# Splitting the first gather of an expert layer: table rows early, token numbers and gathers later

## The chip, the cores and the metric

The kernel runs on 1 core of one Trainium2 chip. The metric is device microseconds (us) of one execution. The core has five engines with an instruction list each: TensorE (PE in the profile; its weight loads are PEld), VectorE (DVE), ScalarE (ACT), GpSimd (POOL) and SyncE (SP, whose queue of transfers is SPq). An engine works through its own list in order and waits on semaphores for the others. A transfer that a later instruction on the same list needs is therefore also a wait for everything behind that instruction.

## The reference

Three layers are computed, all in float32, on 1536 tokens of 512 numbers.

```
x = attention(q, k, v)            # a band of 32 keys, and 24 block sums, per head
x = leaky(x @ w_in) @ w_out       # "first MoE": 512 -> 2048 -> 512, leaky(h) = max(0.01 h, h)
noisy = x @ w_gate + log1p(exp(x @ w_noise)) * noise
top2 = the two largest of the 8 experts for each token, weights = softmax of the two
out[token] += weight * (relu(x[token] @ w1[e]) @ w2[e])     # "second MoE", for both experts
```

The second MoE needs x gathered by expert: which tokens an expert has is known only once the routing of these tokens is done.

## The kernel before, in words

**First MoE.** The 1536 tokens are six groups of 256 (g = 0 to 5) and the 2048 hidden columns are 16 blocks of 128 (f). One pair (g, f) is a step; there are 96, and the last group, g = 5, is steps 80 to 95. Of one step, `l1` (L412) does 12 matmuls into a PSUM bank H0 or H1 (by the parity of f) and the leaky maximum (L424 on ACT, L426 on DVE); `l1b` (L429) cuts the result in two parts, `gh` by ACT (L433) and the rest `gl = t - gh` (L434) by GpSimd or VectorE; `l2` (L437) adds it into the accumulators `acc` with six matmuls, two with gh and one with gl for each half of the tokens. On TensorE the six of step s come after the twelve of step s+2. Which engine makes gl is a table entry: `e_gl<step>=1` is GpSimd from SBUF, 0 is VectorE, in place in the PSUM bank (L425, L434), which is then free for step s+2 only once gl is made.

**Routing.** When a group is through, `x2_out` writes its rows to DRAM (`x2d`, L454), `route_a` transposes them, `route_b` computes the two top experts, and `route_c` (L519) computes a place for each token and scatters (token number, weight) into a table in DRAM, `tabd`, with four indirect transfers that GpSimd issues (L545). The table was filled with a large number before.

**Second MoE.** Work comes in units of 210 or 420 table rows. The first, unit 0, is 210 rows of expert 0, and it takes tokens of groups 0 to 4 only: an offset (`route_off`, L553) keeps the last group's tokens out of its rows. `gather` (L781) loads a unit's rows of the table with a transfer on SP (L785, tile `tbs`), makes valid token numbers `gi` of them on GpSimd (L787), and gathers the tokens' rows with indirect transfers that GpSimd issues (L794, tile `xg`). `xg_t` (L806) transposes them, and `m1` (L817) is the first matmul of the expert. Its weights come by `load_piece` (L161): a 512 KB load on SP into one of three buffers (L171, L173), then a split into two parts, the high one by ACT (L156), the low one by VectorE (L157). The eight pieces of expert 0 are called e01 (first matrix) and e02 (second).

**What sets the order.** Before the last part, each piece of work is put at a step number, a float, by `at_step` (L579); the numbers are the table `PL` (L44). Work is issued in the order of these numbers, and a scheduler places it from there on each engine's list. `xo`, `ra`, `rb`, `rc` are the steps of `x2_out` and the three routing parts of a group, counted from the group's end; `lp` those of the weight pieces. So what an engine does next is fixed when the program is built, and a late semaphore holds everything behind it.

In the rows below, tiles have no numbers; in the lists of instructions `gl_7`, `gh_10`, `lt_9`, `h_11` are those of column block 7, 10, 9, 11 of group 5, that is of steps 87, 90, 89 and 91.

Of the kernel before, what the change touches and what calls it, by code (L numbers as in the profile page):

```python
# [31 lines left out]
NG = N // G  # L32
NT = N // P
NF = FF // P
# [34 lines left out]
          e_gl49=1, e_gl5=1, e_gl50=1, e_gl51=0, e_gl52=0, e_gl53=1, e_gl54=1, e_gl55=1, e_gl56=0, e_gl57=1, e_gl58=1,  # L69
          e_gl59=0, e_gl6=1, e_gl60=0, e_gl61=1, e_gl62=0, e_gl63=0, e_gl64=1, e_gl65=0, e_gl66=1, e_gl67=1, e_gl68=1,  # L70
          e_gl69=0, e_gl7=1, e_gl70=1, e_gl71=0, e_gl72=1, e_gl73=0, e_gl74=1, e_gl75=1, e_gl76=0, e_gl77=0, e_gl78=1,
          e_gl79=0, e_gl8=1, e_gl80=1, e_gl81=0, e_gl82=1, e_gl83=1, e_gl84=0, e_gl85=1, e_gl86=0, e_gl87=1, e_gl88=1,
          e_gl89=1, e_gl9=1, e_gl90=1, e_gl91=1, e_gl92=1, e_gl93=0, e_gl94=1, e_gl95=0, e_kr0=1, e_kr1=1, e_kr2=1,
          e_kr3=1, e_lo0=0, e_lo1=0, e_lo10=1, e_lo11=0, e_lo12=0, e_lo13=0, e_lo14=0, e_lo15=0, e_lo16=1, e_lo17=0,
          e_lo18=0, e_lo19=1, e_lo2=1, e_lo20=0, e_lo21=1, e_lo22=1, e_lo23=1, e_lo24=1, e_lo25=1, e_lo26=1, e_lo27=1,
          e_lo28=1, e_lo29=0, e_lo3=1, e_lo30=1, e_lo31=1, e_lo4=1, e_lo5=1, e_lo6=0, e_lo7=1, e_lo8=1, e_lo9=1,
# [8 lines left out]
          go50=-6.482, go51=-1.899, go52=7.046, go53=-0.034, kt00=1, kt01=0, kt10=1, kt100=1, kt101=1, kt11=1,  # L85
          kt110=0, kt111=0, kt120=0, kt121=0, kt130=1, kt131=0, kt20=1, kt21=0, kt30=1, kt31=0, l1b=2.039, l2=2.48,
          lp0=79.959, lp1=91.15, lp2=94.615, lp3=98.503, lp4=86.197, lp5=99.558, lp6=93.633, lp7=104.712, lw=-6.736,
          lws=0.593, lx=6.628, lxs=0.591, ra0=3.084, ra1=4.274, ra2=4.727, ra3=3.079, ra4=3.418, rb0=8.597, rb1=6.781,
          rb2=9.519, rb3=4.048, rb4=4.635, rc0=15.468, rc1=11.776, rc2=13.732, rc3=6.323, rc4=6.881, tg10a=2, tg10b=2,
          tg10c=3, tg10d=1, tg10e=3, tg11a=1, tg11b=2, tg11c=0, tg11d=3, tg11e=3, tg12a=1, tg12b=2, tg12c=0, tg12d=2,  # L90
          tg12e=2, tg13a=0, tg13b=2, tg13c=3, tg13d=2, tg13e=1, tg20a=1, tg20b=1, tg20c=1, tg20d=1, tg20e=0, tg21a=0,
          tg21b=0, tg21c=1, tg21d=0, tg21e=1, tg22a=0, tg22b=0, tg22c=1, tg22d=1, tg22e=0, tg23a=1, tg23b=1, tg23c=0,
# [4 lines left out]
          tgW16=0, tgW17=1, tgW18=0, tgW19=1, tgW2=0, tgW20=1, tgW21=8, tgW22=8, tgW23=8, tgW24=1, tgW25=0, tgW26=0,  # L97
          tgW27=8, tgW28=8, tgW29=8, tgW3=8, tgW30=8, tgW31=8, tgW4=8, tgW5=8, tgW6=8, tgW7=0, tgW8=8, tgW9=8, vl=0,
          w0=12, wk0=1, wk1=2, wk2=1, wk3=10, x0=-49.567, xo0=1.881, xo1=-22.198, xo2=3.458, xo3=-4.929, xo4=-10.997,
          xo5=5.591)  # L100


C_ID, C_MASK, C_IOTA, C_THR = 0, 128, 128 + 3 * NK, 136 + 3 * NK
# [24 lines left out]
def attention_moe_kernel(ctx: ExitStack, tc: tile.TileContext, q, k, v, w_in, w_out, w_gate, w_noise, noise, w1, w2,  # L128
# [390 lines left out]
    def route_c(g):  # L519

        written.add(("r", g))
        xi, oh, sel, pl, gate, sl = rt.pop(g)
        ps = bank("R", f"pos{g}")
        nc.tensor.matmul(ps[:, :E], tri, sel[:, 0, :], start=True, stop=False)
        nc.tensor.matmul(ps[:, :E], ones, selp, start=False, stop=True)
        nc.tensor.matmul(ps[:, E:2 * E], tri, sel[:, 1, :], start=True, stop=False)
        nc.tensor.matmul(ps[:, E:2 * E], ones, sel[:, 0, :], start=False, stop=False)
        nc.tensor.matmul(ps[:, E:2 * E], ones, selp, start=False, stop=True)
        nc.vector.tensor_scalar(sl[:, 1, :], sl[:, 0, :], 1.0, 1e-9, op0=ALU.add, op1=ALU.add)
        nc.vector.reciprocal(gate[:, :, 0], sl[:, 1, :])  # L530
        nc.vector.tensor_mul(gate[:, :, 1], gate[:, :, 0], sl[:, 0, :])
        nc.gpsimd.tensor_copy(pl[:, :, :, 0], tid[:, 2 * g:2 * g + 2, None].to_broadcast([P, 2, 2]))
        pos = ps[:, :2 * E].rearrange("p (t e) -> p t e", t=2)
        if g == NG - 1:
            pf = rp.tile([P, 2, E], F32, tag="pf", name="pf")
            nc.vector.tensor_add(pf, pos, off[:, None, :].to_broadcast([P, 2, E]))
            pos = pf
        nc.vector.tensor_mul(oh, oh, pos[:, :, None, :].to_broadcast([P, 2, 2, E]))
        nc.vector.tensor_reduce(sl[:, 2:4, :].rearrange("p a b -> p (a b)").rearrange("p (t k) -> p t k", t=2), oh, axis=AX.X, op=ALU.add)
        si = rp.tile([P, 2, 2], I32, tag="si", name=f"si{g}")  # L540
        nc.vector.scalar_tensor_tensor(si, xi, float(TS), sl[:, 2:4, :], op0=ALU.mult, op1=ALU.add)
        done = []
        for t in range(2):
            for j in range(2):
                i = nc.gpsimd.indirect_dma_start(out=tabd, out_offset=IOA(ap=si[:, t, j:j + 1], axis=0), in_=pl[:, t, j, :],  # L545
                                                 in_offset=None)
                for d in done:
                    tc.declare_no_dep(i.ins, d.ins, reason="every token and expert has a table row of its own")
                done.append(i)
        for t in range(2):  # L550
            nc.vector.tensor_add(selp, selp, sel[:, t, :])
# [27 lines left out]
    def at_step(s, fn, *args):  # L579
        events.setdefault(s, []).append((fn, args))  # L580
# [189 lines left out]
        at_step(PL[f"lp{i}"], load_piece, 0, i)  # L770
    at_step(20, routing_consts)
    at_step(48, zero_out)
    at_step(NG * NF - 9, route_off)

# [1 line left out]
    ex = {}  # L778
    mp = None

    def gather(u):  # L781
        e, r0, nj = units[u]
        assert all(("r", g) in written for g in range(NG - 1 + (u > 0)))
        tb = tbs[:, u, :nj, :]
        nc.sync.dma_start(tb, tabd[e * TS + r0:e * TS + r0 + nj * SLOTS, :].rearrange("(p j) c -> p j c", j=nj))  # L785
        gi = rp.tile([SLOTS, nj], I32, tag="gi", bufs=3, name=f"gi{u}")
        nc.gpsimd.tensor_scalar(gi, tb[:, :, 0], (N if u else N - G) - 1, None, op0=ALU.min)  # L787
        if u:
            x = mp.tile([SLOTS, nj, DM], F32, tag="xg", name=f"xg{u}")
        else:  # L790
            x = pa.tile([SLOTS, nj, DM], F32, tag="qn", bufs=1, name=f"xg{u}")
        xg = [x[:, j, :] for j in range(nj)]
        for j in range(nj):
            nc.gpsimd.indirect_dma_start(out=xg[j], out_offset=None, in_=x2d if u else x2d[:N - G, :], in_offset=IOA(ap=gi[:, j:j + 1], axis=0))  # L794
        ex[u] = dict(tb=tb, gi=gi, xg=xg, e=e, nj=nj, n=nj * SLOTS)
# [92 lines left out]
            tc.declare_no_dep(i.ins, o.ins, reason="an expert has each token once")  # L888
        d["out"].append(i)

    at_step(NG * NF - 7, gather, 0)
    for c in range(KD):
        at_step(NG * NF - 4 + c, xg_t, 0, c)

    pool_free = False
    for s in sorted(events):
# [30 lines left out]
    m1(0, 2)  # L927
    second(0, 1)
    route_c(last)
    gather(1)  # L930
    m1(0, 3)
    second(0, 2)
# [12 lines left out]
    for u in range(1, nu):  # L945
        end = u == nu - 1
        for f in range(NFE):
            m1(u, f)
            if f == 0 and not end:
                gather(u + 1)  # L950
            if units[u][0] + 1 < E and f < 7:
                load_piece(units[u][0] + 1, f)
            if f == 1 and u > 1:
                second(u - 1, NFE - 1)
                if not rows[u - 1]:
                    out_sb(u - 1)
# [97 lines left out]
```

## Time and profile before

| | |
|---|---|
| time, median of 3 runs | 745.65 us (741.72 to 747.62) |
| time of the profiled execution | 744.94 us |
| span of that execution, first to last instruction | 743.2 us |
| PE busy | 717.1 us, 96% of the span |
| DVE busy | 391.0 us, 53% |
| ACT busy | 302.3 us, 41% |
| POOL busy | 212.7 us, 29% |
| granted TensorE clock, mean | 0.994 of full speed |
| chain of work that ended last, by engine | PE 82%, DMA 5%, DVE 4%, POOL 3% |

Busy shares are means over the whole span. The profiled execution is one; its time has the 1.74 us around its span in it. PE is busy nearly all the time and carries 82% of the chain that ends last, so what can be won without taking matmuls away is where PE stands still, or runs at a lower granted clock.

### The profile page before, as it was taken

What the parts mean: (1) busy time and instruction counts of PE and PEld (TensorE: products, weight loads), DVE (VectorE), ACT (ScalarE), POOL (GpSimd) and SP (SyncE); (2) the same over time, 40 slices, a digit from 0 to 9 for tenths busy, and PEclk for the clock granted to TensorE, in tenths of its full rate; (3) what the DMA queues carried; (4) which work ended last, traced back from release to release, by engine and by line L of the source; (5) the groups of instructions that cost most, each with busy time, mean ns of one, the idle gap of its engine ahead of it and who ended that gap; (6) DMA issues with size and microseconds to landing.
All of it is one profiled execution on the core that took longest, in us unless ns stands there. A gap on an engine that the chain in (4) does not pass through costs nothing.

```text
span 743.2 us, 13515 instructions
## 1 busy us (share of the span) xinstructions
PE 717.1 (96%) x5240; PEld 633.0 (85%) x5240; DVE 391.0 (53%) x967; ACT 302.3 (41%) x727; POOL 212.7 (29%) x237
## 2 busy tenths in 40 slices
PE   7999999999999999999979999999999999999996
PEld 4577888777888888889869879999999999999984
DVE  3989979855533553332434455455454645454311
ACT  2568656644424544333344145332423333343210
POOL 0212722621143113131240242333324232233132
PEclk9999999999999999999989999999999999999999
DMA  9986454472630120100241257655555546563021
GB/s 249 250 237 179 85 155 163 122 161 50 199 54 30 30 54 2 58 1 1 86 138 56 88 178 233 191 140 161 171 171 163 184 143 182 168 180 124 12 79 48
DMA packets 78993, 92.41 MB, mean 124 GB/s; under 512 B 45254, under 2 KB 54982, under 8 KB 78920
## 3 DMA queue, kind: packets, MB, share of 16 engines
q1 hardware_dynamic: 70728, 72.13, 34.8%
q0 software_dynamic: 8192, 19.33, 8.7%
q8 instruction: 43, 0.70, 0.4%
q14 instruction: 30, 0.25, 0.1%
HBM read 78.62 MB, written 13.40 MB: 124 GB/s over the span
## 4 chain that ended last, share of the span: by engine, by line
PE 82%; DMA 5%; DVE 4%; POOL 3%; ACT 2%; issue 2%; SPq 2%; POOLq 0%; DVEq 0%; ACTq 0%
PE eh L827 19%; PE h L421 16%; PE acc L446 15%; PE eacc L846 15%; PE eacc L866 5%; PE sps L335 2%; DMA early<-in_moe_w_in_dram 2%; PE xgps L813 2%; PE yps L878 1%; PE vps L371 1%; PE aps L356 1%; DMA vn<-in_v_dram 1%; PE vsps L273 1%; PE lg L479 1%; POOL tabd L545 1%
## 5 line engine op out<-in xcount | busy, mean ns | idle before, releaser
L830 ACT ACTIVATE egh<-eh 128x420 fp32r<-128x420 f32 (+1 forms) x72 | 34.7, 482 | 187.6 <-PE eh L827 181.5
L831 DVE SCALAR_TENSOR_TENSOR egl<-eh,egh 128x420 fp32r<-128x420 f32 (+1 forms) x72 | 39.3, 546 | 126.9 <-ACT egh L830 120.9
L434 POOL TENSOR_TENSOR gl<-lt,gh 128x256 fp32r<-128x256 f32 x63 | 47.8, 763 | 167.1 <-ACT gh L433 139.4
L424 ACT ACTIVATE lt<-h 128x256 f32<-128x256 f32 x96 | 36.4, 381 | 68.8 <-PE h L421 59.6
L885 POOL DMA_INDIRECT out_dram<-ag,tbs x32 | 31.9, 996 | 112.5 <-DVE ag L884 100.7
L421 PE MATMUL h<-xh,w0h 128*128 128x256 f32 x192 | 56.2, 293 | 0.5 <-ACT w0h L156 0.4
L421 PE MATMUL h<-xh,w16h 128*128 128x256 f32 x192 | 55.8, 291 | 0.7 <-DVE lt L426 0.4
L421 PE MATMUL h<-xl,w0h 128*128 128x256 f32 x192 | 55.0, 287 | 0.0
L421 PE MATMUL h<-xl,w16h 128*128 128x256 f32 x192 | 54.9, 287 | 0.0
L421 PE MATMUL h<-xh,w16l 128*128 128x256 f32 x192 | 54.7, 285 | 0.0
L421 PE MATMUL h<-xh,w0l 128*128 128x256 f32 x192 | 54.2, 283 | 0.5 <-POOL w0l L157 0.5
L794 POOL DMA_INDIRECT xg<-x2d,gi x32 | 35.8, 1118 | 50.4 <-PE xgps L813 41.9
L426 DVE TENSOR_TENSOR lt<-h,lt 128x256 f32<-128x256 f32 x63 | 26.5, 420 | 40.0 <-ACT lt L424 37.3
L446 PE MATMUL acc<-w17h,gl 128*128 128x512 f32 x96 | 39.2, 408 | 6.1 <-POOL gl L434 5.3
L342 ACT ACTIVATE sm<-sm,st 128x120 f32<-128x120 f32 x96 | 36.8, 385 | 16.8 <-DVE st L340 16.7
L433 ACT ACTIVATE gh<-lt 128x256 fp32r<-128x256 f32 x63 | 26.1, 415 | 37.0 <-PE acc L446 29.2
L802 POOL DMA_INDIRECT ag<-out_dram,gi x28 | 31.8, 1134 | 32.8 <-DMA out_dram<-ag,tbs 19.4
L446 PE MATMUL acc<-w1h,gh 128*128 128x512 f32 x96 | 39.6, 414 | 0.0
L421 PEld LDWEIGHTS h<-xh,w16h 128*128 128x128 f32 x192 | 36.7, 191 | 3.4 <-DVE lt L426 0.9
L446 PE MATMUL acc<-w17h,gh 128*128 128x512 f32 x96 | 39.4, 410 | 0.0
L421 PEld LDWEIGHTS h<-xh,w0h 128*128 128x128 f32 x192 | 36.2, 188 | 3.7 <-DVE lt L426 0.6
L446 PE MATMUL acc<-w17l,gh 128*128 128x512 f32 x96 | 38.8, 404 | 0.0
(304 smaller groups left out, 2092.9 us busy)
## 6 DMA issues: line engine op xcount, KB each, us to landing
e<-in_moe_w_dram SPq DMA_DIRECT2D x64, 512.0 KB
early<-in_moe_w_in_dram SPq DMA_DIRECT2D x8, 512.0 KB
early<-in_moe_w_out_dram SPq DMA_DIRECT2D x8, 512.0 KB
raw<-in_moe_w_in_dram SPq DMA_DIRECT2D x8, 512.0 KB
raw<-in_moe_w_out_dram SPq DMA_DIRECT2D x8, 512.0 KB
vw<-in_v_dram SPq DMA_DIRECT2D x20, 192.0 KB
vn<-in_v_dram SPq DMA_DIRECT2D x8, 384.0 KB
qn<-in_q_dram SPq DMA_DIRECT2D x12, 256.0 KB
```

The costliest lines, as they stand in the source:

```text
L342: nc.scalar.activation(sm[:, i, :], sm[:, i, :], AF.Exp, bias=st[:, i:i + 1], scale=-1.0, accum_out=st[:, 4 + i:5 + i])
L421: nc.tensor.matmul(ps[:, :G], a[:, c, c0:c0 + P], x[:, c, :], start=n == 0, stop=n == 3 * KD - 1)
L424: nc.scalar.activation(t, ps[:, :G], AF.Copy, scale=0.01)
L434: (nc.gpsimd if PL[f"e_gl{g * NF + f}"] else nc.vector).tensor_sub(gl, t, gh.bitcast(F32))
L446: nc.tensor.matmul(accs[g, t], a[:, t * P:(t + 1) * P], w[:, f % 8, :], start=f == 0 and n == 0, stop=f == NF - 1 and n == 2)
L794: nc.gpsimd.indirect_dma_start(out=xg[j], out_offset=None, in_=x2d if u else x2d[:N - G, :], in_offset=IOA(ap=gi[:, j:j + 1], axis=0))
L827: nc.tensor.matmul(ps[:, :w], a[:, c, f * P:(f + 1) * P], x[:, c, :], start=n == 0, stop=n == 3 * KD - 1)
L830: nc.scalar.activation(gh, ps[:, :w], AF.Relu)
L831: nc.vector.scalar_tensor_tensor(gl, ps[:, :w], 0.0, gh.bitcast(F32), op0=ALU.max, op1=ALU.subtract)
L846: nc.tensor.matmul(ps, a[:, f, c * P:(c + 1) * P], x, start=f == 0 and n == 0, stop=f == NFE - 1 and n == 2)
L866: nc.tensor.matmul(d["acc", j][:SLOTS, :], a[:, j * SLOTS:(j + 1) * SLOTS], w[:, f, :], start=f == 0 and n == 0, stop=f == NFE - 1 and n == 2)
L885: i = nc.gpsimd.indirect_dma_start(out=out, out_offset=IOA(ap=d["tb"][:, j, 0:1], axis=0), in_=y, in_offset=None, bounds_check=N - 1, oob_ ...
```

## The change

`gather` is cut in two. The new function `table` holds the load of the table rows on SP; `gather` keeps the token numbers and the gathers on GpSimd. For the first unit, the table load is put at step 87.2 and the gather at step 90.2; both were at step 89 before. For the other units the two are called one after the other, as before. With it go changes in the table of numbers: the three routing parts of group 4 (`ra4`, `rb4`, `rc4`) are put 0.8 to 1.1 steps earlier, `route_off` at 86.6 (was 87), the four `xg_t` of the first unit at 92.6, 93.4, 94.2 and 95.0 (were 92 to 95), and the gl of steps 87, 88 and 89 is made by VectorE.

```diff
-          ... e_gl86=0, e_gl87=1, e_gl88=1,
-          e_gl89=1, ...
+          ... e_gl86=0, e_gl87=0, e_gl88=0,
+          e_gl89=0, ...
-          ... ra4=3.418, ... rb4=4.635, ... rc4=6.881, ...
+          ... ra4=2.6, ... rb4=3.7, ... rc4=5.8, ...
-          xo5=5.591)
+          xo5=5.591, ro=86.6, tb=87.2, ga=90.2, xg=92.6, xgs=.8)
...
-    at_step(NG * NF - 9, route_off)
+    at_step(PL["ro"], route_off)
...
-    def gather(u):
+    def table(u):
+
         e, r0, nj = units[u]
         assert all(("r", g) in written for g in range(NG - 1 + (u > 0)))
         tb = tbs[:, u, :nj, :]
         nc.sync.dma_start(tb, tabd[e * TS + r0:e * TS + r0 + nj * SLOTS, :].rearrange("(p j) c -> p j c", j=nj))
+
+    def gather(u):
+
+        e, r0, nj = units[u]
+        tb = tbs[:, u, :nj, :]
         gi = rp.tile([SLOTS, nj], I32, tag="gi", bufs=3, name=f"gi{u}")
         nc.gpsimd.tensor_scalar(gi, tb[:, :, 0], (N if u else N - G) - 1, None, op0=ALU.min)
...
-    at_step(NG * NF - 7, gather, 0)
+    at_step(PL["tb"], table, 0)
+    at_step(PL["ga"], gather, 0)
     for c in range(KD):
-        at_step(NG * NF - 4 + c, xg_t, 0, c)
+        at_step(PL["xg"] + PL["xgs"] * c, xg_t, 0, c)
...
     route_c(last)
+    table(1)
     gather(1)
...
+                table(u + 1)
                 gather(u + 1)
```

How this stands on the engines' lists. GpSimd, from the scatter of group 4's table rows (L545) on, before:

```order
L545 DMA tabd<-pl_4558,si_4632 13312x2 x4
L434 TENSOR_TENSOR gl_7_4719<-lt_7_4653,gh_7_4720 128x256
L434 TENSOR_TENSOR gl_8_4745<-lt_8_4684,gh_8_4746 128x256
L787 TENSOR_SCALAR gi_4714<-tbs 105x2
L794 DMA xg_4716<-x2d,gi_4714 105x512 x2
L434 TENSOR_TENSOR gl_9_4771<-lt_9_4710,gh_9_4772 128x256
L434 TENSOR_TENSOR gl_10_4808<-lt_10_4742,gh_10_4809 128x256
```

and after the change:

```order
L434 TENSOR_TENSOR gl_5_4661<-lt_5_4575,gh_5_4662 128x256
L545 DMA tabd<-pl_4532,si_4600 13312x2 x4
L793 TENSOR_SCALAR gi_4744<-tbs 105x2
L800 DMA xg_4746<-x2d,gi_4744 105x512 x2
L434 TENSOR_TENSOR gl_10_4801<-lt_10_4737,gh_10_4802 128x256
L434 TENSOR_TENSOR gl_11_4834<-lt_11_4768,gh_11_4835 128x256
```

The first gl behind the token numbers and the gathers was that of step 89; it is that of step 90 now, and between the scatter and the token numbers GpSimd has nothing else.

SP's list around the table load (4630, 4775, 4849, 4884 are pieces of expert 0's weights), the piece of the difference:

```order
-L173 DMA e_4610<-in_moe_w_dram 128x2x512
+L173 DMA e_4630<-in_moe_w_dram 128x2x512
 L171 DMA e_4775<-in_moe_w_dram 128x1024
+L786 DMA tbs<-tabd 105x4
 L173 DMA e_4849<-in_moe_w_dram 128x2x512
-L785 DMA tbs<-tabd 105x4
 L171 DMA e_4884<-in_moe_w_dram 128x1024
```

The table load, which waits for the scatter, stands ahead of weight piece 4849 now, and behind it before.

ACT's list after the change, around weight piece 4884:

```order
L433 ACTIVATE gh_9_4772<-h_9_4698 128x256
L156 ACTIVATE e02h<-e_4849 128x1024
L424 ACTIVATE lt_10_4737<-h_10_4724 128x256
L156 ACTIVATE e01h<-e_4884 128x1024
L433 ACTIVATE gh_10_4802<-lt_10_4737 128x256
L424 ACTIVATE lt_11_4768<-h_11_4755 128x256
```

These six stand in the order that they had before, but that a weight piece has come between lt of block 11 and its gh (the next row): the high part of piece 4884 is ahead of gh of step 90 in both. The gh of step 89 is read from PSUM now.

## Rows read from the trace of the kernel before

**Rows 1.** The longest wait of PE: line, waited for; us, times, longest.

```profile
PE acc L446 <- POOL gl L434: 5.3, 1, 5.3
```

**Rows 2.** The timeline of PE: start us, us, instruction; first of each step.

```profile
376.96 0.28 PE L421 MATMUL h<-xh,w16h 128*128 128x256 f32 x1
...
379.78 0.28 PE L421 MATMUL h<-xh,w16h 128*128 128x256 f32 x1
...
381.21 0.39 PE L446 MATMUL acc<-w17h,gh 128*128 128x512 f32 x1
381.44 0.40 PE L446 MATMUL acc<-w17l,gh 128*128 128x512 f32 x1
387.18 0.79 PE L446 MATMUL acc<-w17h,gl 128*128 128x512 f32 x1 [5.34 <-POOL gl L434]
...
389.05 0.41 PE L421 MATMUL h<-xh,w16h 128*128 128x256 f32 x1
...
393.78 0.28 PE L421 MATMUL h<-xh,w16h 128*128 128x256 f32 x1
...
396.80 0.28 PE L421 MATMUL h<-xh,w16h 128*128 128x256 f32 x1
```

**Rows 3.** Windows: us, then busy (x count) by engine, PEclk, DMA share, GB/s.

```profile
388.00:392.00 4.00, 4.00 (x18) 3.71 (x18) 1.75 (x2) 2.41 (x4) 0.74 (x1) 0.50 0.01 2
...
430.50:431.00 0.50, 0.09 (x1) 0.10 (x2) 0.00 (x0) 0.00 (x0) 0.00 (x1) 1.00 0.00 0
```

**Rows 4.** The timeline of POOL, the scatter, the token numbers and the gathers.

```profile
369.64 1.01 POOL L545 DMA_INDIRECT tabd<-pl,si  x1 [2.96 <-DVE si L541]
...
373.49 1.02 POOL L545 DMA_INDIRECT tabd<-pl,si  x1 [0.30 <-issue]
...
382.13 0.23 POOL L787 TENSOR_SCALAR gi<-tbs 105x2 int32<-105x2 int32 x1 [6.17 <-DMA tbs<-tabd]
...
386.38 1.42 POOL L434 TENSOR_TENSOR gl<-lt,gh 128x256 fp32r<-128x256 f32 x2
...
421.11 0.97 POOL L545 DMA_INDIRECT tabd<-pl,si  x1 [0.30 <-issue]
425.31 0.22 POOL L787 TENSOR_SCALAR gi<-tbs 105x2 int32<-105x2 int32 x1 [3.23 <-DMA tbs<-tabd]
```

**Rows 5.** The timeline of SP's queue: when each transfer was issued.

```profile
372.24 0.38 SPq L173 DMA_DIRECT2D e<-in_moe_w_dram  x1
378.51 0.36 SPq L785 DMA_DIRECT2D tbs<-tabd  x1
378.98 0.81 SPq L171 DMA_DIRECT2D e<-in_moe_w_dram  x2
...
423.66 4.31 SPq L785 DMA_DIRECT2D tbs<-tabd  x8
```

**Rows 6.** The timeline of ACT: high part of a weight piece, then gh.

```profile
383.20 1.06 ACT L156 ACTIVATE e01h<-e 128x1024 fp32r<-128x1024 f32 x1 [3.69 <-DMA e<-in_moe_w_dram]
384.17 0.40 ACT L433 ACTIVATE gh<-lt 128x256 fp32r<-128x256 f32 x1
```

**Rows 7.** The timeline of DVE: low parts of weight pieces, a maximum, a gl.

```profile
135.06 0.69 DVE L157 TENSOR_TENSOR w16l<-raw,w16h 128x512 fp32r<-128x512 f32 x1
...
368.66 0.42 DVE L434 TENSOR_TENSOR gl<-h,gh 128x256 fp32r<-128x256 f32 x1
...
373.64 0.42 DVE L426 TENSOR_TENSOR lt<-h,lt 128x256 f32<-128x256 f32 x1
...
378.02 2.48 DVE L157 TENSOR_TENSOR e02l<-e,e02h 128x1024 fp32r<-128x1024 f32 x2 [1.35 <-ACT e02h L156]
...
384.29 1.23 DVE L157 TENSOR_TENSOR e01l<-e,e01h 128x1024 fp32r<-128x1024 f32 x1 [3.46 <-ACT e01h L156]
```

**Rows 8.** The timeline of POOL: gl beside VectorE, and gl alone.

```profile
135.21 1.13 POOL L434 TENSOR_TENSOR gl<-lt,gh 128x256 fp32r<-128x256 f32 x1 [2.33 <-DVE sm L350]
...
389.39 0.74 POOL L434 TENSOR_TENSOR gl<-lt,gh 128x256 fp32r<-128x256 f32 x1 [1.59 <-ACT gh L433]
```

More of the change, by code (lines that the diff above doesn't have):

```diff
@@ L71 @@
           e_gl69=0, e_gl7=1, e_gl70=1, e_gl71=0, e_gl72=1, e_gl73=0, e_gl74=1, e_gl75=1, e_gl76=0, e_gl77=0, e_gl78=1,
-          e_gl79=0, e_gl8=1, e_gl80=1, e_gl81=0, e_gl82=1, e_gl83=1, e_gl84=0, e_gl85=1, e_gl86=0, e_gl87=1, e_gl88=1,
-          e_gl89=1, e_gl9=1, e_gl90=1, e_gl91=1, e_gl92=1, e_gl93=0, e_gl94=1, e_gl95=0, e_kr0=1, e_kr1=1, e_kr2=1,
+          e_gl79=0, e_gl8=1, e_gl80=1, e_gl81=0, e_gl82=1, e_gl83=1, e_gl84=0, e_gl85=1, e_gl86=0, e_gl87=0, e_gl88=0,
+          e_gl89=0, e_gl9=1, e_gl90=1, e_gl91=1, e_gl92=1, e_gl93=0, e_gl94=1, e_gl95=0, e_kr0=1, e_kr1=1, e_kr2=1,
           e_kr3=1, e_lo0=0, e_lo1=0, e_lo10=1, e_lo11=0, e_lo12=0, e_lo13=0, e_lo14=0, e_lo15=0, e_lo16=1, e_lo17=0,
@@ L87 @@
           lp0=79.959, lp1=91.15, lp2=94.615, lp3=98.503, lp4=86.197, lp5=99.558, lp6=93.633, lp7=104.712, lw=-6.736,
-          lws=0.593, lx=6.628, lxs=0.591, ra0=3.084, ra1=4.274, ra2=4.727, ra3=3.079, ra4=3.418, rb0=8.597, rb1=6.781,
-          rb2=9.519, rb3=4.048, rb4=4.635, rc0=15.468, rc1=11.776, rc2=13.732, rc3=6.323, rc4=6.881, tg10a=2, tg10b=2,
+          lws=0.593, lx=6.628, lxs=0.591, ra0=3.084, ra1=4.274, ra2=4.727, ra3=3.079, ra4=2.6, rb0=8.597, rb1=6.781,
+          rb2=9.519, rb3=4.048, rb4=3.7, rc0=15.468, rc1=11.776, rc2=13.732, rc3=6.323, rc4=5.8, tg10a=2, tg10b=2,
           tg10c=3, tg10d=1, tg10e=3, tg11a=1, tg11b=2, tg11c=0, tg11d=3, tg11e=3, tg12a=1, tg12b=2, tg12c=0, tg12d=2,
```

## The prediction

> **What bounds the kernel now.** I read the waits of PE first. By the page PE is busy 96% of the span, so only its standstills and its clock can be won. The longest is one wait of 5.3 us for a gl of GpSimd [rows 1]. The timeline of PE shows where: step 91 starts at 379.78, and the matmul that needs gl of step 89 starts at 387.18 after 5.34 us of idle [rows 2]. A step takes 379.78 - 376.96 = 2.82 us; this one lasted until 389.05, that is 9.27. The next took 393.78 - 389.05 = 4.73, though its like, with the same two transposes, takes 396.80 - 393.78 = 3.02 [rows 2]. The windows say why: from 388 to 392 the granted clock was 0.50 (1.2 of 2.4 GHz), after the idle time [rows 3]. So the stall costs (9.27 - 2.82) + (4.73 - 3.02) = 6.45 + 1.71 = **8.16 us**, clock included.
>
> Then I asked what GpSimd did. It waited 6.17 us for the table rows, made gi at 382.13, issued two gathers, and came to the gl at 386.38 [rows 4]. Its last scatter started at 373.49 [rows 4], SP issued the table load at 378.51 [rows 5]: 5.02 us for the scatter to land, then 3.62 for the load. The second unit shows the same chain where no weight load lies between: 423.66 - 421.11 = 2.55 and 425.31 - 423.66 = 1.65 [rows 4, 5].
>
> **The change, part by part.** *Removed:* the stall, as long as its cover holds. gl of steps 87 to 89 no longer waits for GpSimd; the first gl behind the gathers is that of step 90. Without a stall step 92 starts at 379.78 + 2.82 = 382.60, and what follows it keeps the distances of step 91: the first matmul of the second layer, which needs gh, came 381.21 - 379.78 = 1.43 after, the next 0.23 later, and the third, which needs gl, was due another 0.23 later [rows 2]. So **gl of step 90 is wanted at 384.50** and its gh at 384.03.
>
> *Is GpSimd free by then?* The routing of group 4 goes one step up: in TensorE's list its matmuls stand one step earlier, and the VectorE chain behind them is as long. The scatters then start near 369.64 - 2.82 = 366.8 and the last, 373.49 - 369.64 = 3.85 later, at 370.7 [rows 4]. With the longest durations shown (5.02, 3.62, and 386.38 - 382.13 = 4.25 from gi to the end of the gathers [rows 4]) GpSimd is free at 383.6; with the shortest (2.55, 1.65, and 4.25) at 379.1. I take the short ones, nearest because weight piece 4849 now stands behind the table load on SP; both are in time. That half of the change does what it says.
>
> *Moved on SP:* piece 4849 was issued at 372.24 [rows 5] and now waits for the table load, to 373.3 or, at the longest, 375.7. A piece needed 383.20 - 378.98 = 4.22 us from issue to the start of its split [rows 5, 6], so it is there by 377.5 to 379.9. Behind it on ACT is the leaky part of step 90, which frees the bank for step 92 at 382.60; 1.06 of split and about 1 of leaky maximum fit. Cost 0, covered by step 91's matmuls; if that cover is gone, each us later is a us of PE.
>
> *What is late next:* piece 4884. It takes the buffer of a piece whose low part ends at 378.02 + 1.2 = 379 in both versions [rows 7], because that part waits for step 87's last matmul, which the change doesn't move. So it is issued near 378.98 and its split starts near 383.20, as before [rows 5, 6]. ACT makes gh of step 90 only behind it, at 384.17 to 384.57 [rows 6]: 0.54 us after PE wants it. Before, this was hidden in the stall.
>
> *And the gl behind that gh:* at 384.29 VectorE starts the low part of the same piece, 1.23 us [rows 7], and gl of step 90 on GpSimd would start at 384.6, beside it. A row shows what that does: the gl at 135.21, begun while a VectorE split ran from 135.06 to 135.75, took 1.13 instead of 0.74 [rows 7, 8], so it ended 0.6 after the split. By this, gl of step 90 ends at 385.52 + 0.6 to 0.74 = 386.1 to 386.26, and PE, which wants it at 384.50, stands **1.7 us**. If the two did not meet, it would end at 384.57 + 0.74 = 385.3, a stall of 0.8. I take 1.7, since the row is of the same pair of operations.
>
> The Trainium skill has a rule for it (SBUF — State Buffer, section Who interferes with whom): a VectorE instruction with two SBUF inputs and a GpSimd instruction that reads SBUF exclude each other, and the second to issue waits for the whole of the first. By that rule the sum is a gain of 6.4 us; by separate ports it would be 7.4. The row at 135.21 is on the rule's side, and it speaks against this change, since it now brings the two together.
>
> *A stall of 1.7 us and the clock:* at 430.5 to 431 PE was idle most of the time and the granted clock stayed 1.00 [rows 3]; I take no drop. If it dropped as before, 1.71 more.
>
> *Three gl on VectorE, in place in the PSUM bank:* 3 subtractions of 0.42 [rows 7], and the bank is free later. That of step 87 stands behind the maximum that ran from 373.64 to 374.06 [rows 7], so it is done by 374.5. PE wants the bank for step 89, at 376.96 - 2.82 = 374.14, or 0.46 later, since TensorE's list now has two matmuls of step 87 ahead. Cost 0, at worst 0.4. The three that GpSimd loses save nothing that waits. The routing matmuls, the transposes and the xg_t are as many as before, in other places: 0. The gathered rows are wanted at 386 and were issued by 379 to 383: 0.
>
> **Sum:** 744.94 (the profiled execution) - 8.16 + 1.7 = 738.5 us. That execution is 0.71 below the median of the runs shown, 745.65, and these lie 5.9 apart, so the base itself is uncertain by some 2 us.
>
> **Rivals.** *Nothing is left of the stall.* Piece 4884 lands a us sooner, since no table load is issued just before it and the gathers are through, and gl slips in ahead of the split. For it: the table load at 378.51 is gone. Against: its issue is tied to the same split. 744.94 - 8.16 = 736.8. Chance 0.25.
>
> *The weights are the new wait, by more than I count.* The gathers (430 KB by their shapes) now run ahead of or beside pieces 4849 and 4884, and the three pieces crowd. If 4884 comes 2 us later, the stall is 3.7 and the clock drops for 1 more: gain 3.5, 741.4. For it: two pieces are issued back to back at 378.98 already [rows 5]. Against: the gathers should be done by then. Chance 0.2.
>
> *Slower: the table load blocks SP.* SP holds piece 4849 until the scatters have landed. In the order before, 4849 was out of the way. If a scatter took long, 4849, then the leaky part of step 90, then step 92 wait, one for one. It loses where the wait passes the 8.16 less the clock's share, 6.4: 4849 would have to land after about 387, its issue at 383, the scatter 12 us after its start. With 8 us of wait and the clock's 1.7: 744.94 - 8.16 + 9.7 = 746.5. Against: 5.02 is the longest shown. Chance 0.05.
>
> *The change doesn't do what it says:* the scheduler could have left gl of step 89 behind the gathers. The lists exclude that; the time would be 745. No chance of its own.
>
> **How the numbers follow.** Forecast 738.5, chance 0.5, its own range 737 to 740 (stalls of 0.3 to 3). The range takes the first rival with its 736.8 and most of the second with 741.4, and adds the base's uncertainty at the low end in part: 735.0 to 742.0. About 1% is what a measurement of this kernel can tell from no change; against 745.65 that is 738.2, close to the forecast. Faster by over 1%: nearly all of the first rival and two fifths of the forecast, 0.43. Within 1%: the rest of both, the second rival and the last one's near end, 0.54. Slower by over 1% would be past 753: 0.03, the last rival's far end and what I have not seen.
>
> **What would show it.** In the profile after: no wait of PE for gl of step 89; gi on GpSimd at 375 to 379; gh of step 90 behind the split of piece 4884 at about 384.5; a PE wait of 0.8 to 2 us for gl of step 90 that ends with the low part of 4884; a granted clock of 1.00 throughout that stretch; all that follows earlier by 6 to 7 us. I am wrong if PE waits in step 92 itself (a bank, so piece 4849), if the clock falls again, or if steps 88 to 90 are longer than 2.82 us.

## The result and the profile after

The changed kernel takes 737.71 us (median of 11 runs, 734.57 to 740.82) against 745.25 (11 runs, 741.72 to 750.98): ratio **0.9897, 95% interval 0.987 to 0.9924**, a gain of 7.7 us give or take 2. The profiled execution took 738.8 us, its span is 736.9, the mean granted clock 0.993.

The timeline of PE (start us, us, instruction) in the place of [rows 2]: the first matmuls of steps 91, 92 and 93, and before the last of them the first matmul with gl of step 90.

```profile
377.62 0.28 PE L421 MATMUL h<-xh,w16h 128*128 128x256 f32 x1
...
380.44 0.28 PE L421 MATMUL h<-xh,w16h 128*128 128x256 f32 x1
...
382.33 0.39 PE L446 MATMUL acc<-w17h,gl 128*128 128x512 f32 x1
...
383.38 0.36 PE L421 MATMUL h<-xh,w16h 128*128 128x256 f32 x1
```

The two steps last 2.82 and 2.94 us. The matmul of gl, which had waited 5.34 us in [rows 2], follows its neighbour without a bracket behind it. The windows (us; busy us of PE, PEld, DVE, ACT, POOL; granted clock, DMA share, GB/s), in the place of [rows 3], say the same of the whole stretch: PE busy 22.00 of 22.00, clock 1.00.

```profile
374.00:396.00 22.00, 22.00 (x139) 19.59 (x138) 11.34 (x20) 12.02 (x25) 8.16 (x6) 1.00 0.39 123
```

GpSimd, in the place of [rows 4]: last scatter, token numbers, second gather, gl of step 90.

```profile
368.57 0.96 POOL L545 DMA_INDIRECT tabd<-pl,si  x1 [0.30 <-issue]
373.69 0.23 POOL L793 TENSOR_SCALAR gi<-tbs 105x2 int32<-105x2 int32 x1 [4.16 <-DMA tbs<-tabd]
...
376.04 1.88 POOL L800 DMA_INDIRECT xg<-x2d,gi  x1 [0.31 <-issue]
379.11 1.53 POOL L434 TENSOR_TENSOR gl<-lt,gh 128x256 fp32r<-128x256 f32 x1 [1.19 <-ACT gh L433]
```

SP, in the place of [rows 5]: the table load, piece 4849, then piece 4884 (the first of the two in the last row).

```profile
370.80 0.36 SPq L786 DMA_DIRECT2D tbs<-tabd  x1
371.26 0.38 SPq L173 DMA_DIRECT2D e<-in_moe_w_dram  x1
371.75 5.69 SPq L171 DMA_DIRECT2D e<-in_moe_w_dram  x2
```

ACT and VectorE, in the place of [rows 6, 7]: the two parts of piece 4884, and gh of step 90 between them.

```profile
377.66 1.06 ACT L156 ACTIVATE e01h<-e 128x1024 fp32r<-128x1024 f32 x1 [0.34 <-DMA e<-in_moe_w_dram]
378.63 0.40 ACT L433 ACTIVATE gh<-lt 128x256 fp32r<-128x256 f32 x1
```

```profile
378.82 1.22 DVE L157 TENSOR_TENSOR e01l<-e,e01h 128x1024 fp32r<-128x1024 f32 x1
```

Three things are to be seen. The last scatter landed in 370.80 - 368.57 = 2.23 us, where it had taken 5.02 [rows 4, 5]. Piece 4884 was issued at 371.75 and its split began at 377.66; in [rows 5, 6] it was 378.98 and 383.20. And gl of step 90 took 1.53 us, beside the low split that runs from 378.82 to 380.04, but it ended at 380.64 and PE wanted it at 382.33.

**The measure for what follows** is the stretch from ACT's copy of group 4's rows (L452) to that of group 5's. It holds steps 80 to 95 and nothing else, so it does not carry the differences of several us that whole executions have. Before and after:

```profile
351.39 0.60 ACT L452 ACTIVATE x<-acc 128x512 f32<-128x512 f32 x1 [0.24 <-PE acc L446]
...
405.16 0.60 ACT L452 ACTIVATE x<-acc 128x512 f32<-128x512 f32 x1 [1.94 <-PE acc L446]
```

```profile
349.03 0.60 ACT L452 ACTIVATE x<-acc 128x512 f32<-128x512 f32 x1 [0.24 <-PE acc L446]
...
394.85 0.60 ACT L452 ACTIVATE x<-acc 128x512 f32<-128x512 f32 x1 [1.94 <-PE acc L446]
```

That is 53.77 before and 45.82 after: **7.95 us gained of the 8.16 that the stall was priced at.** From the first matmul of step 91 (379.78 in [rows 2], 377.62 after) to the end of the stretch it is 25.38 and 17.23, 8.15 gained; the other 0.20 was lost ahead of step 91. Ahead of the stretch this execution was 2.36 us sooner (349.03 to 351.39), where the two kernels do the same work in the same order; behind it, from the copy to the end of the span, it took 736.9 - 394.85 = 342.05 us, and the execution before 743.2 - 405.16 = 338.04. So 4.0 us were lost later. The waits of PE (us in total, times, longest) from 415 to 430 show where most of that is:

```profile
PE xgps L819 <- DMA xg<-x2d,gi: 2.1, 2, 1.1
```

```profile
421.50:428.50 7.00, 6.10 (x28) 5.66 (x29) 3.41 (x8) 2.67 (x6) 2.52 (x4) 0.55 0.13 37
```

These are the transposes of the second unit's rows. In the execution before the same wait was 0.55 us and the clock stayed at 1.00 [rows 3]; here PE stood 2.1 us and then ran at half clock.

### The profile page after: what moved, and what is told of

Read it like the earlier page. It is cut to its first block, busy times and chain, and to the rows that moved or that the text cites. A ratio compares the mean times of both kernels' runs of the same rounds, so it can differ in the third digit from the quotient of the medians.

```text
span 736.9 us, 13516 instructions
## 1 busy us (share of the span) xinstructions
PE 717.0 (97%) x5240; PEld 633.3 (86%) x5240; DVE 392.6 (53%) x970; ACT 301.9 (41%) x727; POOL 211.9 (29%) x234
## 5 line engine op out<-in xcount | busy, mean ns | idle before, releaser
L446 PE MATMUL acc<-w1l,gh 128*128 128x512 f32 x96 | 38.3, 399 | 0.0
```

The lines of the kernel that those rows point to most:

```text
L446: nc.tensor.matmul(accs[g, t], a[:, t * P:(t + 1) * P], w[:, f % 8, :], start=f == 0 and n == 0, stop=f == NF - 1 and n == 2)
```

## The experiments

All times are ratios to the kernel before, run on the same chip, with 95% intervals. The stretch comes from each run's profile. "Landing" is the time from the start of the last scatter to the issue of the table load that waits for it; "load" from there to the start of gi. Where an edit adds lines, the line numbers in the rows are shifted by a few. Stretch, landing and load are of one profiled execution each.

| run | what it is | ratio | stretch | landing | load |
|---|---|---|---|---|---|
| before | | 1 | 53.77 | 5.02 | 3.62 |
| after | | 0.9897 (0.987, 0.9924) | 45.82 | 2.23 | 2.89 |
| again | after, unaltered | 0.9876 (0.9853, 0.9898) | 46.28 | 2.31 | 3.17 |
| gl_only | before, three gl to VectorE | 0.9981 (0.9966, 0.9996) | 52.18 | 4.77 | 2.62 |
| ahead | before, table load ahead of 4849 | 0.9923 (0.9907, 0.9939) | 48.54 | 2.83 | 1.63 |
| late_ahead | after, routing late, order on SP kept | 0.989 (0.9864, 0.9917) | 46.09 | 2.98 | 1.62 |
| behind | after, table load behind 4849 | 0.9931 (0.9911, 0.9951) | 47.72 | 2.17 | 5.27 |
| gl_back | after, three gl on GpSimd | 0.9974 (0.9952, 0.9995) | 50.35 | 2.52 | 2.89 |
| pad256 | after, 1 MB ahead of 4884 | 0.9916 (0.9887, 0.9945) | 47.60 | 2.14 | 3.70 |
| hold | after, next piece ahead of 4884 | 0.9914 (0.9885, 0.9943) | 46.88 | 2.34 | 3.61 |
| hold_dve | hold, gl of step 90 on VectorE | 0.9862 (0.9833, 0.9891) | 45.83 | 2.48 | 3.26 |
| hold_dve_again | the same | 0.9888 (0.986, 0.9915) | 45.82 | 2.30 | 3.16 |
| gl3_dve | after, gl of steps 90 to 92 on VectorE | 0.9939 (0.9916, 0.9962) | 47.06 | 2.12 | 3.32 |
| warm | after, matmuls of no use in unit 1's wait | 0.9872 (0.9847, 0.9897) | 45.84 | 2.48 | 2.94 |

My theory after the result: two things had to go, GpSimd's list being blocked by the wait for the table, and piece 4884 being held on SP by the same wait. Its rivals: moving the three gl was enough, or the order of the two transfers on SP was.

**1. One part alone: the three gl.**

```diff
 (before)
-          e_gl87=1, e_gl88=1, e_gl89=1
+          e_gl87=0, e_gl88=0, e_gl89=0
```

> The kernel before with only gl of steps 87 to 89 moved to VectorE; table load, routing and gather stand as before. Measure: the stretch from ACT's copy of group 4's rows to that of group 5's, 53.77 us before, 45.82 after. Theory (two conditions must hold: GpSimd through with the gathers, and weight piece 4884 early; the earlier routing gives both): the gathers still end at about 386.4, so gl of step 90, wanted at 384.5, ends at about 387.1; a stall of 2.6 to 3.3 stays, with or without the clock's 1.7: stretch 48.2 to 50.6, time ratio to before 0.992 to 0.996. Rival (moving the three gl is all the change needs): stretch 45.8, ratio 0.989. Rival (the gl move gives nothing without the rest): stretch 53.8, ratio 1.000.

GpSimd, token numbers and the first gl behind the gathers; then SP, piece 4849 and the table load; then PE.

```profile
381.36 0.26 POOL L787 TENSOR_SCALAR gi<-tbs 105x2 int32<-105x2 int32 x1 [6.36 <-DMA tbs<-tabd]
...
384.70 1.39 POOL L434 TENSOR_TENSOR gl<-lt,gh 128x256 fp32r<-128x256 f32 x1
```

```profile
372.73 0.38 SPq L173 DMA_DIRECT2D e<-in_moe_w_dram  x1
378.74 0.36 SPq L785 DMA_DIRECT2D tbs<-tabd  x1
```

```profile
388.48 1.00 PE L813 MATMUL xgps<-cst,xg 105*128 105x105 f32 x2 [3.81 <-DMA xg<-x2d,gi]
```

The stretch lost only 1.59 us; at 52.18 it is outside the expected 48.2 to 50.6. I had looked for the remaining wait at gl of step 90; it was at the transposes of the gathered rows instead, 3.81 us, and the clock fell (0.50 from 388 to 392). In the kernel before, the rows came just as late, but the stall for gl had hidden it. So the rows themselves were a second thing behind the same table load.

**2. The other part alone: the order of two transfers on SP.** Piece 4849 is made to follow the table load; all else is the kernel before.

```diff
 (before, load_piece; tbl[0] is the table load of unit 0)
+        with tc.issue_after(tbl[0].ins) if (e, i) == (0, 6) else ExitStack():
             nc.sync.dma_start(raw.rearrange(...), w2[...])
```

> The kernel before, but on SP the table load stands ahead of weight piece 4849; no other instruction moves. Theory (in the kernel before the scatter landed late, 5.02 us, because the 512 KB load of piece 4849 ran beside it): the last scatter, at 373.5, lands within 2.2 to 2.9, table load issued at 375.7 to 376.4 (was 378.51), token numbers made at 378.7 to 379.5 (was 382.13), the stall for gl of step 89 shrinks from 5.3 to about 2.2 to 3, the clock still falls: stretch 50.3 to 51.5, ratio to before about 0.996. Rival (the landing time of the scatter does not depend on the load): table load at 378.5 again, stall 5.3 again, piece 4849 lands at about 383 inside the stall: stretch 53.8 or longer, ratio 1.000.

```profile
371.60 1.03 POOL L548 DMA_INDIRECT tabd<-pl,si  x1 [0.30 <-issue]
...
376.06 0.23 POOL L790 TENSOR_SCALAR gi<-tbs 105x2 int32<-105x2 int32 x1 [1.98 <-DMA tbs<-tabd]
...
379.59 0.75 POOL L437 TENSOR_TENSOR gl<-lt,gh 128x256 fp32r<-128x256 f32 x1
```

```profile
374.43 0.36 SPq L788 DMA_DIRECT2D tbs<-tabd  x1
374.89 0.38 SPq L176 DMA_DIRECT2D e<-in_moe_w_dram  x1
```

```profile
380.39 0.50 PE L449 MATMUL acc<-w17h,gl 128*128 128x512 f32 x1 [0.44 <-POOL gl L437]
...
384.39 0.31 PE L816 MATMUL xgps<-cst,xg 105*128 105x105 f32 x1 [0.89 <-DMA xg<-x2d,gi]
```

The rows show on GpSimd the last scatter, the token numbers and gl of step 89, on SP the table load and piece 4849, and on PE the waits that are left: 0.44 for that gl, 0.89 for the gathered rows and, in rows not shown, 0.42 more for these and 0.23 at the first matmul of step 92. **This order alone is worth 5.23 of the 7.95 us**, more than I expected (50.3 to 51.5). From the last scatter to gi it is 4.46 us, where it was 8.64, and piece 4884, behind the table load on SP, was issued at 375.38 (377.3 on the times of the execution before, where it was 378.98); the run does not divide the gain between the two. The 0.23 is the bank of step 92, freed behind the split of piece 4849, which went out at 374.89 here (376.8 on those times): it is the price of moving this piece, which the prediction put at 0 for an issue up to 375.7. The weight piece of 512 KB had been issued at 372.24, ahead of the last scatter's start at 373.49 [rows 4, 5]. With such a load beside it the landing was 5.02 and 4.77 (before, gl_only); in the twelve other profiles it was 2.12 to 2.98.

The Trainium skill (DMA: Bandwidth & Descriptors, section Queues, rings and completion order) says that each DMA engine takes turns, packet by packet, between the queues that have work for it. By that, the scatter on GpSimd's queue and the load on SP's would take turns, and the small one would be stretched. Two landings of 4.8 to 5.0 against twelve of 2.1 to 3.0 agree with the stretching; no run here shows the turns.

**3. The changed kernel with that order put back.** Piece 4849 goes ahead of the table load; on the other engines no instruction moves.

> The changed kernel, but on SP the table load stands behind weight piece 4849, as in the kernel before; no other instruction moves. Theory (collision of the load with the scatter): piece 4849 issued at 370.2, the last scatter, at 368.6, lands after up to 5 us instead of 2.2: table load at 371.5 to 373.6, token numbers at 374.4 to 376.5, the gathers end at 378.7 to 380.8, gl of step 90, wanted at 382.3, is still in time or late by at most 0.5. Stretch 45.8 to 46.4, ratio to before 0.989 to 0.990. So the order on SP should be worth nothing once the routing is early. Rival (the order on SP is what freed piece 4884): 4884 comes late by more than 2 us, PE stands 1 to 2 us for gl of step 90, stretch 47 to 49.

```diff
 (after, table)
+        with tc.issue_after(raws[0, 6][1].ins):      # the load of piece 4849
             nc.sync.dma_start(tb, tabd[...])
```

```profile
369.88 0.38 SPq L169 DMA_DIRECT2D e<-in_moe_w_dram  x1
370.45 0.36 SPq L796 DMA_DIRECT2D tbs<-tabd  x1
```

```profile
375.72 1.19 POOL L803 TENSOR_SCALAR gi<-tbs 105x2 int32<-105x2 int32 x1 [6.48 <-DMA tbs<-tabd]
```

```profile
384.91 0.31 PE L829 MATMUL xgps<-cst,xg 105*128 105x105 f32 x1 [1.64 <-DMA xg<-x2d,gi]
```

The scatter had begun at 368.28 and landed in 2.17; the weight load came 1.6 us after it here, not 1.2 ahead of it. Now the table load itself stood behind 512 KB in SP's queue: 5.27 us until gi. PE waited 1.64 us for the gathered rows. The theory missed. The stretch lies in the rival's range, but by luck: PE did not wait for gl of step 90, as the rival had it, and piece 4884 was not late. The stretch grew by 1.90 us at a place that I had priced at zero, the gathered rows.

**4. The early routing taken back, the order kept.**

```diff
 (after, with the table load ahead of piece 4849 as in run ahead)
-          ra4=2.6, rb4=3.7, rc4=5.8, ro=86.6
+          ra4=3.418, rb4=4.635, rc4=6.881, ro=87
```

> The changed kernel with the routing of group 4 put back to where it was before (ra4, rb4, rc4, ro), but the table load kept ahead of weight piece 4849 on SP. So it is the run ahead with gl of steps 87 to 89 on VectorE and the transposes of the gathered rows 0.6 step later. Theory (the order of table load and weight piece is what counts, the earlier routing is not needed): the waits of PE for gl (0.4) and for the gathered rows (1.3) that were left in ahead go, stretch 45.8 to 46.5 (48.54 in ahead), ratio to before 0.989. Rival (the earlier routing is worth 2 us by itself): stretch 47.5 to 48.5.

```profile
377.48 1.24 POOL L796 TENSOR_SCALAR gi<-tbs 105x2 int32<-105x2 int32 x1 [3.58 <-DMA tbs<-tabd]
```

```profile
385.34 0.32 PE L822 MATMUL xgps<-cst,xg 105*128 105x105 f32 x1 [0.30 <-DMA xg<-x2d,gi]
```

The rows are the token numbers on GpSimd and the one wait of PE that is left, for the gathered rows. The stretch is 46.09, as good as the change but for 0.3, so the earlier routing is not needed for its own sake. What it does in the change is to put the table load ahead of 4849: with the routing late and nothing else altered, the scheduler places the piece first on SP, although `tb` is 87.2. So the parts are worth 1.59 (gl_only) and 5.23 (ahead) by themselves, 7.68 together (late_ahead), and 7.95 with the routing early.

**5. The three gl back on GpSimd.**

```diff
 (after)
-          e_gl87=0, e_gl88=0, e_gl89=0
+          e_gl87=1, e_gl88=1, e_gl89=1
```

> The changed kernel with gl of steps 87 to 89 back on GpSimd. On GpSimd's list gl of step 87 then stands behind the first gather, those of 88 and 89 behind the second. Theory: gl of step 87, wanted at about 373.9, cannot start before about 375.8 and runs beside VectorE's split from 375.86, so it ends at about 377.5: a stall of 3.6, with the clock's drop up to 5.3; the two gl behind it are then in time. Stretch 45.8 + 3.6 to 5.3 = 49.4 to 51.1, ratio to before 0.994 to 0.997. Rival (the earlier routing alone frees GpSimd, the gl move was not needed): stretch 45.8, ratio 0.989.

```profile
377.78 1.06 POOL L800 DMA_INDIRECT xg<-x2d,gi  x1 [0.76 <-POOL gi L793]
378.88 0.73 POOL L434 TENSOR_TENSOR gl<-lt,gh 128x256 fp32r<-128x256 f32 x1
```

```profile
379.66 0.79 PE L446 MATMUL acc<-w1h,gl 128*128 128x512 f32 x1 [2.85 <-POOL gl L434]
```

The first gather and gl of step 87 behind it, then PE. The stretch is as expected, 50.35, the ratio, 0.9974, just past the expected 0.997: PE waited 2.85 us, not 3.6, and the clock fell, to 0.57 from 379 to 383. The three gl on VectorE are a condition of moving the gather's place, and by themselves worth little (1.59 in gl_only).

**6. Piece 4884 made late,** to see whether the forecast stall comes back.

```diff
 (after, load_piece)
+            pad = dpool.tile([256, 1024], F32, name="pad")
+            r = nc.sync.dma_start(pad, w1[1, :256, :])        # behind piece 4849
+            with tc.issue_after(r.ins):
                 nc.sync.dma_start(raw, w1[0, 2 * P:3 * P, :])   # piece 4884
```

> The changed kernel with a copy of 1 MB that nobody needs (expert 1's weights to a scratch place in DRAM) on SP's queue just ahead of weight piece 4884; the engines' lists are the same. Theory (the stall that was forecast for gl of step 90 is missing only because piece 4884 came at 377.7 instead of about 381): the piece lands 3.5 to 5 us later, at 381.2 to 382.7, gh of step 90 behind its split at 382.2 to 383.8, gl of step 90 on GpSimd locked out by the low split to 384.2 to 385.7; wanted at 382.3, so PE stands 1.9 to 3.4: stretch between the row copies 47.7 to 49.2 (45.82 in the changed kernel), 1 to 1.7 more if the clock falls; ratio to before 0.990 to 0.995. Rival (the piece does not decide): stretch 45.8 to 46.3.

The high part on ACT and the gh behind it, the low part on VectorE, gl on GpSimd, and PE:

```profile
380.91 1.06 ACT L156 ACTIVATE e01h<-e 128x1024 fp32r<-128x1024 f32 x1 [3.60 <-DMA e<-in_moe_w_dram]
381.88 0.40 ACT L441 ACTIVATE gh<-lt 128x256 fp32r<-128x256 f32 x1
```

```profile
382.00 1.23 DVE L157 TENSOR_TENSOR e01l<-e,e01h 128x1024 fp32r<-128x1024 f32 x1 [3.10 <-ACT e01h L156]
```

```profile
382.36 1.45 POOL L442 TENSOR_TENSOR gl<-lt,gh 128x256 fp32r<-128x256 f32 x1 [4.44 <-ACT gh L441]
```

```profile
382.33 0.50 PE L454 MATMUL acc<-w17h,gh 128*128 128x512 f32 x1 [0.30 <-ACT gh L441]
...
383.87 0.51 PE L454 MATMUL acc<-w17h,gl 128*128 128x512 f32 x1 [0.81 <-POOL gl L442]
```

The chain is the one that was forecast, link by link: piece, high part, gh, gl locked out by the low part until 383.81, PE at 383.87. The piece landed at 380.91, a little sooner than I had expected, so PE stood 0.30 + 0.81 = 1.11 us, not 1.9 to 3.4. The stretch is 1.78 longer than after, 47.60 where I had expected 47.7 or more, and the clock stayed at 1.00 (375 to 395).

**7. The two runs hold and hold_dve.** Piece 4884 is put behind the next piece on SP.

```diff
 (after, load_piece; raw3 is the buffer of the next piece)
+            r = nc.sync.dma_start(raw3[0], w1[0, 3 * P:4 * P, :])
+            with tc.issue_after(r.ins):
                 nc.sync.dma_start(raw, w1[0, 2 * P:3 * P, :])
 (hold_dve: besides)
-          e_gl90=1
+          e_gl90=0
```

> The changed kernel, but on SP weight piece 4884 stands behind the next piece, 4939, which has to wait for its buffer until about 377.1; no other instruction moves. So 4884 is issued at about 377.5 (371.75 in the changed kernel) and lands at 381.7 to 383.4. Theory (the time of piece 4884 decides whether a stall for gl of step 90 is left; gl of step 90 on GpSimd is locked out by VectorE's split of the piece): gl of step 90, wanted at 382.3, ends at 384.6 or later: PE stands 2.3 to 4.0, with the clock's drop up to 1.7 more: stretch between the two row copies 48.1 to 51.5 (45.82 in the changed kernel). Without the lock-out 1.5 to 3.2. Rival (the stall went because of the gathers alone, whenever the piece comes): stretch 45.8.

> The kernel of the run hold, with gl of step 90 made by VectorE, ahead of its split of piece 4884. Theory (lock-out): gl of step 90 ends 0.42 after gh instead of 0.6 after the whole low split, so PE stands about 1.1 less than in hold: stretch 1.1 shorter. Rival (no lock-out; GpSimd's gl takes 0.74 beside the split): 0.3 shorter.

These did not do what I meant: the splits changed places with the loads, and gl of step 90 had only the early piece ahead of it. But the late one, issued at 377.97 in hold, now stood ahead of gh of step 91, and there the same chain showed: high part at 384.40, gl at 385.85 for 1.46 us, PE waiting 0.71 until 387.36. In hold_dve its high part started at 382.50, 1.1 sooner when counted from the start of the stretch, and no such wait was left. So they do not price the lock-out: that hold_dve's stretch is 1.05 shorter, as the theory said (1.1), is luck, since the wait that is gone is another one. The short time of hold_dve, 0.986, did not come again:

> The kernel of the run hold_dve once more, to see whether it beats the changed kernel (ratios to before so far 0.986 from 4 runs against 0.988 and 0.990). Theory (its stretch between the row copies, 45.83, is that of the changed kernel, 45.82 and 46.28; its shorter time was chance): ratio 0.988 to 0.990, stretch 45.8 to 46.3. Rival (gl of step 90 on VectorE takes away a wait that comes in some executions): ratio 0.985 to 0.987.

Its second ratio is 0.9888 and the stretch 45.82: not told apart from the changed kernel.

**8. No gl on GpSimd there at all.**

```diff
 (after)
-          e_gl90=1, e_gl91=1, e_gl92=1
+          e_gl90=0, e_gl91=0, e_gl92=0
```

> The changed kernel with gl of steps 90 to 92 on VectorE as well, so that no gl of GpSimd stands beside a VectorE split of expert 0's weights. Theory (in the changed kernel this lock-out is hidden but for 0 to 0.7 us at gl of step 91): stretch 45.8, no wait of PE for gl, ratio to before 0.985 to 0.990. Rival (in place in the PSUM bank the gl frees the bank too late for the step two later): a wait of PE in h of 0.5 to 1, stretch 46.3 to 46.8.

```profile
387.42 0.41 DVE L434 TENSOR_TENSOR gl<-h,gh 128x256 fp32r<-128x256 f32 x1
```

```profile
387.89 0.38 PE L421 MATMUL h<-xh,w16h 128*128 128x256 f32 x1 [0.99 <-DVE gl L434]
```

The rival was right in its mechanism. gl of step 91 is made in the PSUM bank, behind the low part of piece 4939, and step 93 waits 0.99 us for the bank: the stretch is 1.24 longer than after, a little past the rival's range.

**9. The later loss.** The changed kernel once more, and with matmuls of no use in the wait of unit 1.

> The changed kernel once more, unaltered, to see whether the wait of PE for the gathered rows of the second unit (2.1 us, and half clock behind it) belongs to the change or to that one execution. In the five other profiles (before and four variants) the way from the first result of unit 0 to the first of unit 1 took 26.5 to 26.9 us; in the changed kernel 30.0. Theory (that one execution): 26.5 to 27.2 now, and stretch between the row copies 45.8 again. Rival (it belongs to the change): 29 to 30 again.

```profile
386.20 0.50 PE L446 MATMUL acc<-w17h,gl 128*128 128x512 f32 x1 [0.20 <-POOL gl L434]
```

In again the wait at unit 1 was 0.3 us and the way from unit 0 to unit 1 26.68. So the 2.1 us do not come in every execution. But again lost elsewhere: at unit 2 PE stood 1.75 us for VectorE (444.47), behind a late piece of expert 1. The row is a rest of the forecast chain, a wait of 0.20 for gl of step 91.

```diff
 (after, ahead of xg_t(1, ...))
+    ps = bank("H0", "warm")
+    for _ in range(8):
+        nc.tensor.matmul(ps[:, :2 * SLOTS], ew[0, 1][0][:, 0, :P], ex[0]["x"][0][:, 0, :], start=True, stop=True)
```

> The changed kernel with eight matmuls of no use (128x210, 0.11 us each) on TensorE ahead of the transposes of unit 1's rows, where it waits 0.8 to 2.1 us for them. Theory: they lie inside the wait and keep the clock at 1.00 where it would fall: 0 to 3 us gained in executions with a long wait, nothing in others; ratio to before 0.986 to 0.990. Rival (the wait is mostly shorter than 0.9): up to 0.4 us lost, ratio 0.990 to 0.991.

```profile
420.01 1.04 PE L951 MATMUL warm<-exh,e01h 128*128 128x210 f32 x8
421.30 0.28 PE L819 MATMUL xgps<-cst,xg 105*128 105x105 f32 x1 [0.24 <-DMA xg<-x2d,gi]
422.58 0.49 PE L819 MATMUL xgps<-cst,xg 105*128 105x105 f32 x3 [1.00 <-DMA xg<-x2d,gi]
```

```profile
424.00:426.00 2.00, 2.00 (x12) 2.00 (x11) 1.05 (x3) 0.69 (x2) 0.27 (x1) 0.50 0.00 0
```

Here the wait was long again, so it is not of one execution alone. The eight matmuls filled its first 1.04 us; 0.24 and 1.00 were left, and the clock fell all the same, to 0.50 from 424 to 426. The theory that they would keep it at 1.00 missed. The time is that of again: no gain that can be measured.

What stays open: from group 5's copy to the end of the span after, again and warm took 342.05, 341.22 and 341.10 us, and the eleven other profiles 337.8 to 338.7. The losses lie at different places (unit 1 in after and warm, unit 2 in again), and behind and pad256 have the same lists there as after and again. I have no cause for it. If each execution of the changed kernel had it, 3 us would be to be won there. The times rather speak against that: of the eleven of the changed kernel the fastest is 734.57 and the profiled one 738.8, of the six of again the fastest is 735.32 and the profiled one, 738.64, the slowest. Only a profile of a fast one would show it, and there is none.

## Why the prediction was right, step by step

The forecast was 738.5 (735.0 to 742.0); 737.71 was measured. The interval of the ratio is four us wide, so the time alone does not tell the terms apart; the stretch does.

- **The stall is worth 8.16, the clock's share in it.** Right: the stretch gave 7.95 and, in again, 7.49.
- **GpSimd is free at 379.1 to 383.6, before gl of step 90 is wanted.** Right: it was free at 377.92. The whole execution was 2.36 sooner than the one before, so on the times of that execution, which the prediction uses, it is 380.3, about 1.1 behind the short end: the load took 2.89 where I had taken 1.65. That the short durations hold because 4849 stands behind the table load was right, and it was worth more than the place it got: run ahead shows that this order by itself is most of the gain. I counted it as a detail of one duration; it is the main term, and moving the three gl, which I took for the mechanism, is by itself worth 1.59.
- **Piece 4849 later by some us, at no cost.** Right in the changed kernel: it was issued at 371.26 (373.6 on the times of the execution before), its high part started at 376.00, and step 92 did not wait. In ahead, where it went out later, step 92 paid 0.23.
- **What is late next: piece 4884.** *This step failed.* I tied its issue to the split of another piece. The buffer that it takes is that of piece 4775, and it was free sooner: the low part of 4775 had ended at 373.68 before and at 371.61 in the changed kernel. VectorE, before and after:

```profile
372.47 1.21 DVE L157 TENSOR_TENSOR e01l<-e,e01h 128x1024 fp32r<-128x1024 f32 x1
```

```profile
370.39 1.22 DVE L157 TENSOR_TENSOR e01l<-e,e01h 128x1024 fp32r<-128x1024 f32 x1
```

What held the piece until 378.98 in [rows 5] was the table load ahead of it on SP's list, issued at 378.51. With the table load at 370.80, the piece went at 371.75 (374.1 on the times of the execution before), and gh of step 90 was done at 379.03, 2.8 us before PE wanted it (381.87).
- **gl of step 90 locked out by the low part of the piece: a stall of 1.7.** The lock-out is right, 1.53 us instead of 0.74, and it ended 0.60 after the split, as forecast. The stall is not: 1.7 us of slack covered it, since the piece was early. In pad256, with the piece late, the chain gave the stall back. The order can also be the other way round; in again gl began 0.02 before the split, kept its 0.74, and the split took 1.80 instead of 1.22:

```profile
379.08 0.74 POOL L434 TENSOR_TENSOR gl<-lt,gh 128x256 fp32r<-128x256 f32 x1 [0.88 <-ACT gh L433]
```

```profile
379.10 1.80 DVE L157 TENSOR_TENSOR e01l<-e,e01h 128x1024 fp32r<-128x1024 f32 x1
```

The rule of the Trainium skill that the prediction weighed (SBUF — State Buffer, section Who interferes with whom) says that the one that issues first keeps the ports for its whole instruction and the other waits. The two orders here agree with it but for 0.14 us: a wait for the whole of the first would have made the second 1.67 and 1.94 us long, and they took 1.53 and 1.80.
- **No fall of the clock.** Right for this stretch: 1.00.
- **Three gl on VectorE at no cost.** Right here, and gl_back shows that they are needed. The cost in a bank that is free later does exist: gl3_dve paid 0.99 for it.
- **The gathered rows cost nothing.** Right in the changed kernel, but their slack was not what I thought: gl_only paid 3.81 for them, behind 1.64.

So the rival that nothing is left of the stall (736.8, chance 0.25) described this stretch. It named the right transfer, the table load at 378.51, but another reason: the piece was not quicker (5.91 us from issue to split, 4.22 before), it was issued sooner. That the forecast time held although its last term, 1.7 us, did not come is luck: 738.5 and 736.8 both lie within the four us that the measurement leaves open. In the profiled execution, 738.8, two things that I had not counted nearly cancel as well: it was 2.36 sooner ahead of the stretch, and it lost 4.0 us behind it.

## What to carry to other kernels

A small load that waits for something holds all that stands behind it in its queue, and a large load that stands ahead of it, or beside what it waits for, makes it late: place the small one first, and look at both neighbours before any engine's list is changed. When a transfer is late, read what its own queue issued just before it, and not only when its buffer came free. Behind a stall of 5 us other late things are hidden; take each one's slack, not just the one that ends last.

## What was not expected of the hardware

The last of four small scatters landed in 2.1 to 3.0 us, and in 4.8 to 5.0 with a 512 KB load issued 1.2 us before it. A load of 1.6 KB right behind a 512 KB load on the same queue was seen by its reader after 5.27 us (behind, one profile); ahead of it, after 1.6 to 3.7, a spread that I cannot explain. GpSimd's token numbers, 105x2, took 1.19 to 1.24 us in behind and late_ahead instead of 0.23; in both a VectorE split was under way. The issue of the second gather on GpSimd took 0.96 us in gl_only and late_ahead, where no split was under way at its start, and 1.88, 1.52 and 1.28 in after, again and hold_dve, where one had 1.05, 0.69 and 0.44 us left to run. Some stretches grew by 0.25 to 0.35 us more than the wait in them: behind 1.90 with one wait of 1.64, gl3_dve 1.24 with 0.99, hold 1.06 with 0.71, again 0.46 with 0.20; late_ahead did not, 0.27 with 0.30. And a wait's length alone did not say whether the clock would fall: 0.24 and 1.00 us in warm were followed by half clock, 1.64 us in behind and 0.30 and 0.81 in pad256 were not.
